# Attention and experts on one core: own banks for the transposes of single slots, and GpSimd's weight splits placed by the slot that runs

## The chip, the cores and the metric

The kernel runs on 1 core of a Trainium2 chip. The metric is the device time of one execution in microseconds (us). Before the change the median of 3 runs is 1021.44 us (1020.47 to 1024.28).

Engines are named as the profile names them: PE is TensorE (PEld its weight loads), DVE VectorE, ACT ScalarE, POOL GpSimd, SP SyncE; a q behind a name means the engine's queue, which issues DMAs and waits.

## The reference

Attention with rotary positions over 8 x 8 heads of 576 x 64, then a mixture of 8 experts on its 4608 rows of 512. Each row goes to one expert, the one with the largest gate logit:

```python
e_idx = np.argmax(logits, axis=1)
for e in range(E):
    mask = e_idx == e
    h = np.maximum(x[mask] @ w1[e], 0.0)      # 512 -> 1024
    ye = h @ w2[e]                            # 1024 -> 512
    out[mask] = gate_w[mask, None] * eom[mask, e, None] * ye
```

Everything is fp32. The kernel reaches fp32 precision on PE with pairs of a rounded part and its remainder: x = xh + xl, w = wh + wl, and x w is taken as xh wh + xl wh + xh wl.

## The kernel before, in words

Attention takes somewhat more than the first half of the time. The expert part is the class `Moe`. The rows of each expert are cut into **slots**. A double slot holds 256 rows in two halves of 128 and a single slot 128 rows. The list `todo` fixes their order: 26 slots run, numbered 0 to 25, and the singles are 7, 8, 10, 12, 13, 15, 17, 18, 20, 22, 23 and 25; so there are four pairs of singles (7 and 8, 12 and 13, 17 and 18, 22 and 23), three lone singles with a double behind them (10, 15, 20), and the last slot. A further branch for more slots stands behind them.

The weights of a slot come in 8 pieces of 128 x 1024: pieces 0 to 3 are w1, pieces 4 to 7 are w2. Piece j of slot s has the number u = 8 s + j, and the tiles of it are `wr` (loaded), `wh` (rounded part) and `wl` (remainder); wl87 is piece 7 of slot 10.

`slot` (line 1169) writes out the order by hand, in 8 steps, for every engine at once. In step j:

- PE works on piece j. Steps 0 to 3 are `first` (ph, the product with w1, and its relu on ACT), steps 4 to 7 are `second` (py, the product with w2).
- In a single slot relu rows `hr` lie with the tokens on the partitions, so they are turned on PE by `across` (line 1109) in steps 1 to 4: two transposes into `htp`, then ACT rounds them into one half of `ht` and DVE takes the remainder into the other (L1118, L1119). In a double slot L1106 and L1107 do that without a turn.
- `split` (line 1040) is called for piece u + 6: ACT rounds wr to wh (L1047) and one engine takes the remainder wl (L1049). That engine is POOL when the piece is for a single slot and is its piece 1 or 5, and DVE otherwise.
- SP issues the load of piece u + 8 (L1038) as soon as its buffer of eight is read.
- In steps 4 and 5 `turn` brings in the tokens of the next slot: four transposes into `mtp` (L1055), ACT's rounded part and DVE's remainder `xt` (L1070, L1071). A single slot has one such part, a double slot two. The product with w1 of the next slot needs all of `xt`.
- In step 6 POOL issues the gather of the tokens of slot s + 2 (L1025), and in step 7 the stores of this slot's rows (L1144), one for a single and two for a double. A store waits for its rows and for the store before it to land.

So each engine has one queue in the order of these calls, and an instruction waits for all that stand ahead of it on its engine. `Small` hands out PSUM tiles for transposes; in the expert part they come from a pool of two banks, shared by `mtp` and `htp`, and a transpose waits until the tile two before it has been read. `ph` has two banks and the pool `pm` (py) two of four.

```python
eng = self.nc.gpsimd if self.todo[s][0] == 1 and j % 4 == 1 else self.nc.vector   # in split, s and j of the piece
tp = self.small.tile(f"htp{s}_{j}{self.nm}")                                      # in across
self.split(u + self.LEAD)                                                         # in slot, LEAD = 6
```

Of the kernel before, what the change touches and what calls it, by code (L numbers as in the profile page):

```python
# [10 lines left out]
F32 = mybir.dt.float32  # L11
# [12 lines left out]
P = 128  # L24
# [738 lines left out]
class Moe:  # L763
# [273 lines left out]
        self.wr[u] = self.buf("wr", u, self.LOADS, 4, [P, 1024], F32, f"wr{u}{self.nm}")  # L1037
        self.nc.sync.dma_start(out=self.wr[u], in_=self.w[bass.ds(self.regs[s] * P + j * E * P, P), :])  # L1038

    def split(self, u):  # L1040
        if u >= 8 * self.end:
            return
        s, j = divmod(u, 8)
        wh = self.buf("wh", u, self.SPLITS, 3, [P, 1024], F32R, f"wh{u}{self.nm}")
        wl = self.buf("wl", u, self.SPLITS, 3, [P, 1024], F32R, f"wl{u}{self.nm}")
        r = self.wr.pop(u)
        self.nc.scalar.copy(wh, r)  # L1047
        eng = self.nc.gpsimd if self.todo[s][0] == 1 and j % 4 == 1 else self.nc.vector
        eng.tensor_tensor(out=wl, in0=r, in1=wh.bitcast(F32), op=ALU.subtract)  # L1049
        self.wp[u] = (wh, wl)  # L1050

# [58 lines left out]
    def across(self, s, j):  # L1110

        hth, htl = self.ht[s]
        js = slice(2 * j, 2 * j + 2)
        hr = self.hrs.pop((s, j))
        tp = self.small.tile(f"htp{s}_{j}{self.nm}")
        for f in range(2):
            self.nc.tensor.transpose(out=tp[:, f, :], in_=hr[:, f, :], identity=self.ident)
        self.nc.scalar.copy(hth[:, js, 0:P], tp[:, 0:2, :])  # L1118
        self.nc.vector.tensor_tensor(out=htl[:, js, 0:P], in0=tp[:, 0:2, :], in1=hth.bitcast(F32)[:, js, 0:P], op=ALU.subtract)  # L1119
# [51 lines left out]
    def slot(self, s, left, per=2):  # L1171
        for j in range(8):
            u = 8 * s + j
            single = self.todo[s][0] == 1
            if j < 4:
                if s or j > 1 or not self.n0:
                    self.first(s, j)
            else:
                self.second(s, j - 4)
            if single and 1 <= j <= 4:  # L1180
                self.across(s, j - 1)
            self.split(u + self.LEAD)
            self.load(u + self.LOADS)
            if j in (4, 5):
                self.turn(s + 1, j - 4)
            if j == 7:
                self.store(s)
            if j == 6:
                self.gather(s + 2)
            for _ in range(per if s or j > 1 else 1):  # L1190
                if left:
                    left.pop(0)()
# [64 lines left out]
```

## Time and profile before

| | |
|---|---|
| median of 3 runs | 1021.44 us (1020.47 to 1024.28) |
| profiled execution: its time, its span | 1019.95 us, 1018.1 us |
| PE, DVE, ACT, POOL busy over the span | 94%, 80%, 61%, 59% |
| splits of weights on DVE, on POOL | 184, 24 |
[...]

The page gives shares over the whole span, while the change lies in the expert part alone, from about 560 us on. So the table is only a start: what counts is read from single slots, by windows cut at the slots' borders, by what PE waits for there, and by the instructions of DVE, ACT and POOL in order of time.

### The profile page before, as it was taken

The numbers are of one execution on the slowest core, as the hardware profiler recorded it, in microseconds if no ns is written. First come the engines' busy times: TensorE is split into PE (matmuls) and PEld (weight loads), VectorE is DVE, ScalarE is ACT, GpSimd is POOL, SyncE is SP. The second block draws the span as 40 slices with busy tenths as digits, with TensorE's granted clock in tenths as the row PEclk, the third lists the DMA queues.
The fourth block names the chain that finished last, engine by engine and source line by source line (L and its number), as shares of the span: only waits on it lengthen the run. The fifth ranks groups of instructions, "written<-read, shape, count | busy, mean of one in ns | idle before, by whom it ended". The sixth has DMA issues, their size and how long they took to land.

```text
span 1018.1 us, 34712 instructions
## 1 busy us (share of the span) xinstructions
PE 960.7 (94%) x14461; PEld 841.7 (83%) x14461; DVE 812.5 (80%) x1262; ACT 621.2 (61%) x1300; POOL 601.0 (59%) x620
## 2 busy tenths in 40 slices
PE   4999999989999999999889999999999999999995
PEld 4778888878878788887788888898998989898894
DVE  6789989989899999999759777667677776867772
ACT  4566666656666666666545455458567765856762
POOL 4677998898988989989521112135315243542621
PEclk9999999999999999999999999999999999999998
DMA  6555665575746748555569767658787877977860
GB/s 223 158 160 155 185 201 147 168 213 150 230 117 198 212 124 239 168 170 146 183 215 337 269 205 238 219 196 306 284 300 238 332 282 255 348 271 275 288 245 29
DMA packets 58208, 221.00 MB, mean 217 GB/s; under 512 B 9351, under 2 KB 9660, under 8 KB 53952
## 3 DMA queue, kind: packets, MB, share of 16 engines
q1 hardware_dynamic: 50304, 196.37, 60.8%
q0 software_dynamic: 6464, 21.26, 5.4%
q8 instruction: 115, 1.88, 0.8%
q10 hardware_dynamic: 1280, 1.11, 0.3%
q14 instruction: 45, 0.37, 0.1%
HBM read 198.64 MB, written 22.43 MB: 217 GB/s over the span
## 4 chain that ended last, share of the span: by engine, by line
PE 70%; POOL 10%; DVE 8%; issue 6%; ACT 5%; DMA 1%; ACTq 0%; POOLq 0%; SPq 0%; DVEq 0%
PE py L1132 18%; PE sc L491 16%; PE ph L1090 15%; PE acc L533 10%; PE ph L1082 5%; POOL raw L435 4%; PE acc L548 4%; ACT pm L505 3%; DVE m L496 3%; DVE wl L1049 2%; POOL raw L439 2%; PE mtp L1055 2%; POOL q L417 1%; POOL pl L714 1%; ACT wh L1047 1%
## 5 line engine op out<-in xcount | busy, mean ns | idle before, releaser
L505 ACT ACTIVATE pm<-sc,m 128x576 f32<-128x576 f32 x288 | 211.3, 738 | 180.1 <-DVE m L496 176.7
L1049 DVE TENSOR_TENSOR wl<-wr,wh 128x1024 fp32r<-128x1024 f32 x184 | 253.2, 1389 | 44.7 <-ACT wh L1047 43.1
L496 DVE TENSOR_REDUCE m<-sc 128x1 f32<-128x576 f32 x288 | 205.8, 749 | 44.3 <-PE sc L491 43.1
L491 PE MATMUL sc<-kh,q 64*128 64x288 f32 x1024 | 205.3, 324 | 21.4 <-ACT pm L505 9.6
L1132 PE MATMUL py<-wh,ht 128*128 128x512 f32 x640 | 214.3, 399 | 0.0
L1047 ACT CAST wh<-wr 128x1024 fp32r<-128x1024 f32 x208 | 212.5, 1050 | 0.0
L533 PE MATMUL acc<-pt,v 32*64 32x128 f32 (+1 forms) x9216 | 197.2, 296 | 13.0 <-DVE xb L560 8.5
L511 DVE STREAM_TRANSPOSE pt<-pm 128x576 f32<-128x576 f32 x288 | 207.1, 753 | 0.0
L491 PEld LDWEIGHTS sc<-kh,q 64*128 64x128 f32 x1024 | 154.0, 190 | 51.8 <-ACT pm L505 27.7
L533 PEld LDWEIGHTS acc<-pt,v 32*64 32x64 f32 x9216 | 157.8, 131 | 38.3 <-issue 22.2
L435 POOL TENSOR_TENSOR raw<-raw,rt 128x1152 f32<-128x1152 f32 x62 | 164.1, 2647 | 0.2
L1090 PE MATMUL ph<-xt,wh 128*128 128x256 f32 x896 | 160.9, 282 | 0.5 <-DVE xt L1071 0.5
L1090 PEld LDWEIGHTS ph<-xt,wh 128*128 128x128 f32 x896 | 138.2, 189 | 2.7 <-DVE xt L1071 1.5
L1132 PEld LDWEIGHTS py<-wh,ht 128*128 128x128 f32 x640 | 120.2, 188 | 24.0
L491 PE MATMUL sc<-kl,q 64*128 64x288 f32 x512 | 129.7, 306 | 0.0
L1090 PE MATMUL ph<-xt,wl 128*128 128x256 f32 x448 | 125.8, 281 | 0.0
L1132 PE MATMUL py<-wl,ht 128*128 128x512 f32 x320 | 125.0, 391 | 0.0
L1049 POOL TENSOR_TENSOR wl<-wr,wh 128x1024 fp32r<-128x1024 f32 x24 | 58.7, 2444 | 89.0 <-ACT wh L1047 75.2
L439 POOL TENSOR_TENSOR raw<-raw 128x576 f32<-128x576 f32 x62 | 88.0, 1419 | 1.8
L1106 ACT ACTIVATE ht<-ph 128x512 fp32r<-128x512 f32 x56 | 33.5, 598 | 88.0 <-PE ph L1090 88.0
L491 PEld LDWEIGHTS sc<-kl,q 64*128 64x128 f32 x512 | 86.1, 191 | 0.4 <-DVE kl L417 0.2
L1090 PEld LDWEIGHTS ph<-xt,wl 128*128 128x128 f32 x448 | 84.5, 189 | 0.1
(248 smaller groups left out, 1308.2 us busy)
## 6 DMA issues: line engine op xcount, KB each, us to landing
wr<-in_w SPq DMA_DIRECT2D x208, 512.0 KB, 5.3
raw<-in_qk SPq DMA_DIRECT2D x64, 576.0 KB, 4.7
v<-in_v SPq DMA_DIRECT2D x128, 288.0 KB, 5.4
xd<-xb SPq DMA_DIRECT2D x16, 640.0 KB, 6.4
xd<-xb SPq DMA_DIRECT2D x8, 160.0 KB, 4.4
rt<-in_rope ACTq DMA_DIRECT2D x1, 576.0 KB, 5.5
xg<-xd,2idx POOLq DMA_INDIRECT x18, 7.1
out<-y,2idx POOLq DMA_INDIRECT x18, 5.2
```

The lines of the kernel that those rows point to most:

```text
L435: self.eng(eng).tensor_tensor(out=rv, in0=rv, in1=self.rt[:, 2 * t:2 * t + 2, x], op=ALU.mult)
L439: self.eng(eng).tensor_tensor(out=r[:, 2 * t, x], in0=r[:, 2 * t, x], in1=r[:, 2 * t + 1, x], op=ALU.add)
L491: self.nc.tensor.matmul(self.ps[i][:, a, :HS], st, mov[r, x], start=(n == 0), stop=(n == 2))
L496: nc.vector.tensor_reduce(self.m[i], ps[:, :, :HS], axis=AX.XY, op=ALU.max, negate=True)
L505: nc.scalar.activation(pe.rearrange("p (a b) -> p a b", a=2), self.ps[i][:, :, :HS], AF.Exp, bias=self.m[i], scale=1.0, accum_out=self.z[: ...
L511: self.nc.vector.transpose(out=self.pt[:, st[0] + 5 * st[1] if st else 4, :], in_=self.pc.pop(i))
L533: nc.tensor.matmul(self.acc[h * D:h * D + D, a, o:o + 32 * n], self.v[r, h, j, :], self.pt[r, u:u + n, 32 * j:32 * j + 32], start=(j == 0) ...
L1047: self.nc.scalar.copy(wh, r)
L1049: eng.tensor_tensor(out=wl, in0=r, in1=wh.bitcast(F32), op=ALU.subtract)
L1082: nc.tensor.matmul(ph[:, 0, :], st[:, dc, 0:P], mv[:, dc, :], start=(n == 0), stop=(n == 11))
L1090: nc.tensor.matmul(ph[:, f, :], st[:, dc, fs], mv[:, dc, :], start=(n == 0), stop=(n == 11))
L1132: self.nc.tensor.matmul(py[h], st[:, f, hs], mv, start=(f == 0 and n == 0), stop=(f == 7 and n == 2))
```

## The change

It does two things. The transposes of `across` no longer use the two shared banks: they take two tiles, htp0 and htp1, in the pool `pm`, which fills its four banks. And `split` no longer chooses its engine by the slot that the piece is for: POOL takes the remainder in steps 1 and 4 of a single slot that is running, so of its own piece 7 and of piece 2 of the slot behind it.

```diff
-    def split(self, u):
+    def split(self, u, help=False):
...
-        eng = self.nc.gpsimd if self.todo[s][0] == 1 and j % 4 == 1 else self.nc.vector
+        eng = self.nc.gpsimd if help else self.nc.vector
...
-        tp = self.small.tile(f"htp{s}_{j}{self.nm}")
+        tp = self.pm.tile([P, 4, P], F32, tag=f"htp{j % 2}", name=f"htp{s}_{j}{self.nm}")
...
-            self.split(u + self.LEAD)
+            self.split(u + self.LEAD, single and j in (1, 4))
```

POOL's queue from the stores of slot 6 (y6) to that of slot 8 (y8), the first pair of singles. xg is a gather of tokens, out a store.

```order
 L1144 DMA out_0<-y6_12076,2idx_11216 4608x512 x2
-L1049 TENSOR_TENSOR wl65_12190<-wr65_12141,wh65_12189 128x1024
-L1025 DMA xg_9501<-xd_83,2idx_11216 128x640 x2
-L1049 TENSOR_TENSOR wl69_12261<-wr69_12234,wh69_12260 128x1024
+L1049 TENSOR_TENSOR wl63_12138<-wr63_12074,wh63_12137 128x1024
+L1049 TENSOR_TENSOR wl66_12208<-wr66_12167,wh66_12207 128x1024
+L1025 DMA xg_9501<-xd_83,2idx_11216 128x640 x2
 L1144 DMA out_0<-y7_12266,1idx_11566 4608x512
+L1049 TENSOR_TENSOR wl71_12324<-wr71_12264,wh71_12323 128x1024
+L1049 TENSOR_TENSOR wl74_12394<-wr74_12353,wh74_12393 128x1024
 L1025 DMA xg_9501<-xd_83,1idx_11566 128x640
```

In slot 7 the two splits now stand ahead of the gathers for slot 9, with none between these and the store of slot 7, and slot 8, which had no split on POOL, has two. Over all slots POOL has 23 splits and DVE 185.

DVE's queue in slot 10, a lone single, from its step 0 to the second half of slot 11's tokens, as it is with the change.

```order
L1049 TENSOR_TENSOR wl86_12722<-wr86_12669,wh86_12721 128x1024
L1119 TENSOR_TENSOR ht1_10_12705<-htp10_0_12751,ht0_10_12704 128x2x128
L1119 TENSOR_TENSOR ht1_10_12705<-htp10_1_12777,ht0_10_12704 128x2x128
L1049 TENSOR_TENSOR wl88_12783<-wr88_12734,wh88_12782 128x1024
L1119 TENSOR_TENSOR ht1_10_12705<-htp10_2_12803,ht0_10_12704 128x2x128
L1049 TENSOR_TENSOR wl89_12809<-wr89_12760,wh89_12808 128x1024
L1119 TENSOR_TENSOR ht1_10_12705<-htp10_3_12821,ht0_10_12704 128x2x128
L1064 COPY gs11_12834<-xg_9501 128x2
L1071 TENSOR_TENSOR xt1_11_12833<-mtp11_0_12836,xt0_11_12832 128x4x128
L1049 TENSOR_TENSOR wl91_12850<-wr91_12812,wh91_12849 128x1024
L1071 TENSOR_TENSOR xt1_11_12833<-mtp11_1_12855,xt0_11_12832 128x4x128
```

Before, wl87 stood between the first two remainders of relu rows and wl90 ahead of the copy gs11; both are on POOL now. The last instruction shown stands behind wl89 and wl91 as before.

PE in slot 8, where the tokens of slot 9 are turned; the waits are named by engine or DMA queue.

```order
-L1055 MATMUL mtp9_0_12403<-ident_91,xg_9501 128x128 [waits DMASW0_49,DVE_49]
+L1055 MATMUL mtp9_0_12403<-ident_91,xg_9501 128x128 [waits DMASW0_49]
 L1055 MATMUL mtp9_0_12403<-ident_91,xg_9501 128x128 x3
 L1132 MATMUL py8_0_12381<-wh69_12260,ht0_8_12271 128x512
-L1132 MATMUL py8_0_12381<-wl69_12261,ht0_8_12271 128x512 [waits Pool_49]
+L1132 MATMUL py8_0_12381<-wl69_12261,ht0_8_12271 128x512
```

The order of PE's instructions is unchanged. The transposes of tokens wait for the gather alone now, and no longer for DVE to have read a tile of relu rows.

## Rows read from the trace of the kernel before

**Rows 1.** Slots 7 to 10: length, busy us of PE, PEld, DVE, ACT, POOL (instructions)
```profile
689.76:702.35 12.59, 12.59 (x86) 11.47 (x86) 9.09 (x12) 10.74 (x18) 6.24 (x4) 1.00 0.79 267
702.35:716.02 13.67, 13.21 (x90) 11.85 (x90) 12.57 (x16) 12.08 (x20) 6.93 (x4) 1.00 0.99 382
716.02:738.88 22.86, 22.86 (x150) 20.81 (x150) 13.94 (x14) 11.86 (x15) 10.06 (x5) 1.00 0.76 268
738.88:751.87 12.99, 12.99 (x89) 11.65 (x88) 10.59 (x15) 11.18 (x19) 3.04 (x3) 1.00 0.82 289
```
**Rows 2.** Waits of PE and its weight loads, 640 to 1010 us (total, times, longest)
```profile
PE mtp L1055 <- DVE ht L1119: 2.5, 4, 0.8
...
PEld mtp L1055 <- DVE ht L1119: 3.5, 4, 1.1
PEld ph L1090 <- DVE xt L1071: 0.6, 3, 0.2
```
**Rows 3.** Instructions on the tile wl: duration in ns, least, median, most
```profile
L1049 DVE TENSOR_TENSOR wl<-wr,wh x184: 1203/1224/3451, 514.3 to 999.3; 128x1024 fp32r<-128x1024 f32 x184
L1049 POOL TENSOR_TENSOR wl<-wr,wh x24: 2388/2444/2506, 680.0 to 990.1; 128x1024 fp32r<-128x1024 f32 x24
```
**Rows 4.** Order of time, DVE and POOL where their splits meet (start, us, instruction, idle before)
```profile
701.76 2.35 DVE L1049 TENSOR_TENSOR wl<-wr,wh 128x1024 fp32r<-128x1024 f32 x2
703.90 2.47 POOL L1049 TENSOR_TENSOR wl<-wr,wh 128x1024 fp32r<-128x1024 f32 x1
705.21 2.24 DVE L1049 TENSOR_TENSOR wl<-wr,wh 128x1024 fp32r<-128x1024 f32 x1 [1.10 <-ACT wh L1047]
...
684.05 4.55 DVE L1049 TENSOR_TENSOR wl<-wr,wh 128x1024 fp32r<-128x1024 f32 x2
685.08 2.44 POOL L1049 TENSOR_TENSOR wl<-wr,wh 128x1024 fp32r<-128x1024 f32 x1 [0.70 <-ACT wh L1047]
...
953.68 2.45 POOL L1049 TENSOR_TENSOR wl<-wr,wh 128x1024 fp32r<-128x1024 f32 x1
953.87 0.42 DVE L1119 TENSOR_TENSOR ht<-htp,ht 128x256 fp32r<-128x256 f32 x1 [0.71 <-ACT ht L1118]
```
**Rows 5.** Order of time in slot 10: POOL, DVE, ACT, and PE's weight loads
```profile
744.87 0.98 POOL L1144 DMA_INDIRECT out<-y,2idx  x1 [4.65 <-DVE wl L1049]
745.02 1.23 DVE L1049 TENSOR_TENSOR wl<-wr,wh 128x1024 fp32r<-128x1024 f32 x1
746.71 1.23 DVE L1049 TENSOR_TENSOR wl<-wr,wh 128x1024 fp32r<-128x1024 f32 x1
750.00 1.22 DVE L1049 TENSOR_TENSOR wl<-wr,wh 128x1024 fp32r<-128x1024 f32 x1
751.14 0.69 DVE L1071 TENSOR_TENSOR xt<-mtp,xt 128x512 fp32r<-128x512 f32 x1
...
747.11 1.05 ACT L1047 CAST wh<-wr 128x1024 fp32r<-128x1024 f32 x1
...
751.88 0.19 PEld L1090 LDWEIGHTS ph<-xt,wh 128*128 128x128 f32 x1 [0.20 <-DVE xt L1071]
```
**Rows 6.** Order of time in slots 7 and 8: POOL, DVE, ACT
```profile
695.66 0.98 POOL L1144 DMA_INDIRECT out<-y,2idx  x1 [4.57 <-DVE wl L1049]
700.24 1.85 POOL L1025 DMA_INDIRECT xg<-xd,2idx  x1 [0.16 <-issue]
702.39 1.48 POOL L1025 DMA_INDIRECT xg<-xd,2idx  x1 [0.30 <-issue]
706.52 1.82 POOL L1144 DMA_INDIRECT out<-y,1idx  x1 [0.15 <-issue]
...
695.92 1.23 DVE L1049 TENSOR_TENSOR wl<-wr,wh 128x1024 fp32r<-128x1024 f32 x1
...
707.41 1.06 ACT L1047 CAST wh<-wr 128x1024 fp32r<-128x1024 f32 x1
710.61 1.05 ACT L1047 CAST wh<-wr 128x1024 fp32r<-128x1024 f32 x1
```

## The prediction

> **What bounds the kernel now.** The change touches single slots only, so I read the windows cut at the borders of slots 7 to 10 first [rows 1]. PE is busy in all of slot 7 (12.59 of 12.59 us), slot 9 and slot 10, and in 13.21 of 13.67 us of slot 8. So PE sets the pace there, and only slot 8, the second of a pair of singles, has a hole. The reader should also see the columns of DVE: 12.57 of 13.67 us in slot 8 and 10.59 of 12.99 in slot 10, against 13.94 of 22.86 in slot 9, a double. DVE is nearly full exactly where the change adds to what it may have to wait for.
>
> The waits of PE say what the hole is [rows 2]: over all 26 slots PE waits for `mtp` behind DVE's read of a tile of relu rows 4 times, 2.5 us in all, 3.5 us by the weight loads. Four is the number of pairs. Nothing else makes PE wait there but 0.6 us for `xt`, three times 0.2, as at 751.88 ahead of slot 11 [rows 5]. That small row matters: DVE's last piece of the next tokens ended at 751.14 + 0.69 = 751.83 and PE took it at once. Behind a lone single, DVE has no slack left.
>
> **Part 1, the banks.** The transposes of tokens lose their wait for DVE. That takes away 2.5 us if nothing else comes late, 3.5 at most [rows 2]. It adds no instruction. But the tokens' remainder is still taken by DVE in its own order, so the gain holds only if DVE delivers `xt` as much earlier.
>
> [...]
>
> **Part 2, the splits.** A split takes 2.44 us on POOL and 1.22 on DVE [rows 3]. What counts is how they meet [rows 4]:
>
> - A DVE split reached while POOL's runs is held to its end and ends 1.08 us after it: POOL 703.90 + 2.47 = 706.37, DVE 705.21 + 2.24 = 707.45.
> - A POOL split reached while DVE's runs is held likewise and ends 2.26 us after it: the DVE pair of 701.76 ends at 704.11, POOL at 706.37.
> - Who waits first is served first: the second DVE split of the two from 684.05 (4.55 us, against 2.35 for such a pair alone) let the POOL split of 685.08 pass, and lost 2.20 us. I take it that a waiting DVE split likewise passes a second POOL split.
> - DVE instructions that read PSUM are not held: the one at 953.87 took 0.42 us in the middle of a POOL split. These are `ht` and `xt`.
>
> So a POOL split removes 1.14 us from DVE (the step from 750.00 to 751.14 [rows 5]) and costs it up to 2.2 us of waiting if DVE is full. In doubles this was paid out of idle time; there DVE now gets all eight splits and no hold, which costs nothing under 22.86 us of PE [rows 1]. In singles there is no such cover. [...]
>
> *A lone single (slots 10, 15, 20).* I put the new order on the rows of slot 10 [rows 5]. The first POOL split, wl87, stands behind the second store, which ends at 744.87 + 0.98 = 745.85, long after its cast. DVE is in wl88 until 745.02 + 1.23 = 746.25, so wl87 ends at 746.25 + 2.26 = 748.51. wl89, which ran from 746.71, ends at 748.51 + 1.08 = 749.59 instead of 747.94. The second POOL split, wl90, has its cast at 747.11 + 1.05 = 748.16 and waits behind wl89: 749.59 + 2.26 = 751.85. DVE meanwhile does the remainder of relu rows and the first half of the tokens, then reaches wl91 and is held: 752.93 instead of 751.22. The second half of slot 11's tokens follows, 0.08 before that end and 0.69 long: 753.54 instead of 751.83. PE waits **1.7 us**. Three such slots: 5.1 us.
>
> *A pair (7 and 8, and three more).* Same rules [rows 6]. The store ends at 696.64, DVE's wl64 at 695.92 + 1.23 = 697.15, so wl63 on POOL ends at 699.41, wl65 on DVE at 700.49, wl66 on POOL at 702.75, wl67 on DVE at 703.83. That harms nothing in slot 7 itself: the one token half of slot 8 is ready near 701.5, before 702.35. Three more DVE splits of 1.14 bring DVE to 707.25, two remainders of relu rows to 708.0. POOL has the two gathers and the store ahead of its next split: 702.75, and as long as from 700.24 to 703.87, and 1.82, and three gaps of some 0.2 make 708.5. DVE's next split, wl72, has its cast at 707.41 + 1.06 = 708.47. So both arrive together, and there are two cases.
>
> - DVE first: wl72 709.71, wl71 on POOL 711.97, wl73 713.05, wl74 on POOL 715.31, wl75 716.39, the last half of the tokens 717.0.
> - POOL first: wl71 710.90, wl72 711.98, wl74 (cast at 710.61 + 1.05 = 711.66) 714.24, wl73 715.32, the remainder of the relu rows and half the tokens some 0.95, wl75 717.4, the last half 718.0.
>
> Slot 9 began at 716.02 [rows 1], with the `mtp` hole in it. It would begin at 717.0 or 718.0: **1.0 to 2.0 us** later, the gain of part 1 already used up. I take 1.5, the middle, since the tie can fall either way. Four pairs: 6 us.
>
> Slot 25 has one POOL split left and no slot behind it: nothing.
>
> **The sum.** 5.1 + 6.0 = 11.1 us more. The profiled execution took 1019.95 us, so 1031 for it; the median of the runs is 1.5 us above it, 1021.44, so **1032 us**. The ends of the costs: 3 x 1.7 + 4 x 1.0 = 9 and 3 x 1.7 + 4 x 2.0 = 13.
>
> **Rivals.**
>
> *The holes close and nothing opens (not slower).* One mechanism: POOL's splits fall into the time in which DVE waits for casts, DVE has its two splits fewer per single, `xt` comes in time, and PE saves its 2.5 to 3.5 us: 1018 to 1019 us. The place that decides is the last half of the tokens of slot 11: it must be there by 751.9. For it speaks that DVE is idle 2.4 us in slot 10; against it, that this idle time lies ahead of the point where POOL is freed by its store (745.85). [...] 6 in 100.
>
> *Only the second hold counts.* If POOL's second store came some 2 us earlier (its wait there is 4.65 us behind the store before [rows 5]), wl87 would be over early. Then wl90 from 748.16 meets wl89 until 748.4, ends near 750.6, wl91 near 751.7, the tokens near 752.3: 0.5 us a lone single, and nothing or the saved 0.6 in a pair. 1020 to 1024 us. POOL is off PE's path now, so little pulls the store forward: 9 in 100. Something between this and the forecast, 1024 to 1029: 12 in 100.
>
> *POOL's lateness reaches further (worse).* The buffer of slot 7's last piece, wr63, is free when POOL ends at 699.41; before, DVE had read it ahead of wl64, by 695.92 [rows 6]. The load into it, the cast of that piece and ACT's queue behind the cast can shift by up to those 3.5 us, as can the two gathers, now behind wl66. The trace of before has no row in which ACT waits for a load or PE for a gather, so the price lies between 0 and 3.5 us a pair; it decides where the store that frees POOL lands latest. With POOL first in every pair, and half the pairs at the middle of that, 1.7, the sum is 5.1 + 8 + 3.4 = 16.5 us: 1038. 18 in 100.
>
> **How the numbers follow.** The forecast with its own range, 1029 to 1036, has 55 in 100. Half a per cent, 5.1 us, is about what a measurement of this kernel tells from no change. Faster by more than that is out of reach of both parts (at most 3.5 us): 2 in 100, for what I do not see. Within it lie the first two rivals: 15. The rest, 83, is slower. The range that leaves out no more than 2 in 10 runs from 1024, above the first two rivals, to 1041, above the worst.
>
> **What would show it.** In the new profile PE's wait for `mtp` behind DVE is gone. In its place PE waits for `xt` L1071 ahead of the doubles behind singles, seven times, by 1 to 2 us each; POOL's 23 splits lie in single slots, and DVE splits that meet them take up to 3.4 us. Slots 7 and others that are followed by a single keep their length, doubles theirs. It is wrong if DVE's splits in singles are not held, if PE's wait for `xt` stays under 0.5 us in slot 11, or if PE waits for casts or gathers instead.

## The result and the profile after

The changed kernel takes 1033.03 us (median of 6 runs, 1030.97 to 1036.22); the kernel before, run beside it, 1023.33 us (6 runs, 1020.47 to 1027.79). The ratio is **1.0096** (95% interval 1.0067 to 1.0124): 0.7 to 1.2% slower, and the medians differ by 9.7 us. The profiled execution took 1030.97 us with a span of 1029.2, 11.1 us more than the span before, at a mean granted clock of 0.993 (before: 0.997). One run of e1 below took 2976.96 us, far from all others, and is left out there.

To find where, I cut PE's rows at the first product with w1 of each slot. The **expert part**, from slot 0's first product to the last product with w2 of slot 25, took 486.1 us before (520.8 to 1006.9 us of the trace) and 497.0 after: 10.95 of the 11.1 us. The differences in the lengths of slots, after less before:

| slots | first single | second single | double behind | together |
|---|---|---|---|---|
| 7, 8, 9 | -0.04 | -0.27 | +1.29 | +0.98 |
| 12, 13, 14 | -0.02 | -0.30 | +1.41 | +1.09 |
| 17, 18, 19 | -0.03 | -0.63 | +1.43 | +0.77 |
| 22, 23, 24 | -0.02 | -0.65 | +1.52 | +0.85 |
| 10, 11 (lone) | +1.49 | | +2.78 | +4.27 |
| 15, 16 (lone) | -0.01 | | +1.34 | +1.33 |
| 20, 21 (lone) | -0.04 | | +1.66 | +1.62 |

Slots 0 to 6 and 25 differ by 0.05 at most. The windows of slots 7 to 11 of the changed kernel (length, busy us of PE, PEld, DVE, ACT and POOL, granted clock) answer to [rows 1]:

```profile
689.78:702.33 12.55, 12.55 (x86) 11.48 (x84) 8.96 (x10) 10.69 (x18) 7.36 (x5) 1.00 0.64 200
702.33:715.73 13.40, 13.24 (x90) 11.86 (x88) 12.34 (x14) 11.81 (x20) 9.74 (x6) 1.00 0.97 362
715.73:739.88 24.15, 23.05 (x150) 20.73 (x148) 16.56 (x18) 11.90 (x16) 4.18 (x4) 1.00 0.88 314
739.88:754.36 14.48, 13.23 (x89) 11.75 (x88) 10.91 (x11) 11.44 (x19) 8.69 (x5) 1.00 0.50 172
754.36:780.04 25.68, 24.59 (x149) 22.28 (x148) 16.55 (x18) 11.68 (x15) 3.03 (x2) 0.93 0.74 260
```

The hole in slot 8 has shrunk from 0.46 to 0.16 us, and holes have opened in slots 9, 10 and 11. The waits of PE and of its weight loads in the changed kernel, from 640 us on (total, times, longest), say what they are:

```profile
PEld ph L1090 <- DVE xt L1071: 10.8, 7, 1.8
PE ph L1090 <- DVE xt L1071: 8.6, 7, 1.5
...
PE py L1132 <- DVE ht L1119: 1.3, 1, 1.3
PE ph L1082 <- DVE xt L1071: 0.5, 3, 0.2
```

The wait for `mtp` behind DVE [rows 2] is gone. In its place PE waits seven times, once ahead of each double behind a single, for DVE's last half of the tokens. The splits of the changed kernel by engine, beside [rows 3]:

```profile
L1049 DVE TENSOR_TENSOR wl<-wr,wh x185: 1203/1219/3406, 514.8 to 1008.7; 128x1024 fp32r<-128x1024 f32 x185
L1049 POOL TENSOR_TENSOR wl<-wr,wh x23: 2390/2419/2797, 694.8 to 1010.8; 128x1024 fp32r<-128x1024 f32 x23
```

All 23 of POOL's splits now lie in single slots, and 22 of them meet splits of DVE. Sorted by the two rules of the prediction, the rows show one picture: where DVE is held, its end is 1.08 or 1.09 us behind POOL's; where POOL is held, its split ends 2.27 to 2.29 us behind DVE's.

**What the prediction had not seen** stands in the rows of DVE and POOL of the changed kernel at the end of slot 8, in order of time:

```profile
712.31 2.40 POOL L1049 TENSOR_TENSOR wl<-wr,wh 128x1024 fp32r<-128x1024 f32 x1 [2.44 <-ACT wh L1047]
...
712.35 0.41 DVE L1119 TENSOR_TENSOR ht<-htp,ht 128x256 fp32r<-128x256 f32 x1
712.68 2.05 DVE L1064 COPY gs<-xg 128x2 f32<-128x2 f32 x1
714.65 0.68 DVE L1071 TENSOR_TENSOR xt<-mtp,xt 128x512 fp32r<-128x512 f32 x1
715.25 1.21 DVE L1049 TENSOR_TENSOR wl<-wr,wh 128x1024 fp32r<-128x1024 f32 x1
716.38 0.68 DVE L1071 TENSOR_TENSOR xt<-mtp,xt 128x512 fp32r<-128x512 f32 x1
```

DVE's copy of the gates, `gs`, 2 numbers a partition, takes 2.05 us and ends at 714.73, 0.02 behind POOL's split. It stands ahead of both halves of the tokens. The row above it, `ht` from PSUM, is not held (0.41). Over the whole kernel the copy's durations are, before and then after:

```profile
L1064 DVE COPY gs<-xg x26: 152/156/414, 513.0 to 988.5; 128x2 f32<-128x2 f32 x26
```
```profile
L1064 DVE COPY gs<-xg x26: 149/163/2064, 513.5 to 998.3; 128x2 f32<-128x2 f32 x26
```

Ten of the 26 copies take 2.03 to 2.06 us after the change, the others 0.15 to 0.17. Six of the ten stand ahead of a double, in slots 8, 13, 15, 18, 20 and 23; the other four, in slots 7, 12, 17 and 22, stand ahead of a second single, where PE waits 0.2 us at most.

**Slot 10 is a case of its own.** POOL's and DVE's rows of the changed kernel there:

```profile
745.76 2.42 POOL L1049 TENSOR_TENSOR wl<-wr,wh 128x1024 fp32r<-128x1024 f32 x1
749.45 2.41 POOL L1049 TENSOR_TENSOR wl<-wr,wh 128x1024 fp32r<-128x1024 f32 x1 [1.27 <-issue]
...
746.18 3.09 DVE L1049 TENSOR_TENSOR wl<-wr,wh 128x1024 fp32r<-128x1024 f32 x1 [0.53 <-ACT wh L1047]
749.20 0.41 DVE L1119 TENSOR_TENSOR ht<-htp,ht 128x256 fp32r<-128x256 f32 x1
749.53 3.41 DVE L1049 TENSOR_TENSOR wl<-wr,wh 128x1024 fp32r<-128x1024 f32 x1
752.87 0.41 DVE L1119 TENSOR_TENSOR ht<-htp,ht 128x256 fp32r<-128x256 f32 x1
```

POOL came first both times, the second time by 0.08 us (749.45 against 749.53), so DVE lost nearly 2 us and then 2.2. The last remainder of relu rows, at 752.87, is then late as well as the tokens. PE and the windows behind it in the changed kernel:

```profile
753.33 0.74 PE L1132 MATMUL py<-wh,ht 128*128 128x512 f32 x2 [1.25 <-DVE ht L1119]
...
755.73 0.38 PE L1090 MATMUL ph<-xt,wh 128*128 128x256 f32 x1 [1.09 <-DVE xt L1071]
```
```profile
755.50:760.00 4.50, 4.27 (x23) 4.27 (x24) 2.44 (x3) 0.00 (x0) 3.03 (x2) 0.62 0.92 347
760.00:764.00 4.00, 4.00 (x36) 4.00 (x36) 2.17 (x3) 2.41 (x4) 0.00 (x0) 1.00 0.62 245
```

PE was idle for 1.25 and for 1.09 us within 4 us, and from 756.0 to 759.4 us the granted clock stood at 0.5 of full speed; in the 4.5 us of the first window that leaves a mean of 0.62, and 0.38 x 4.5 = 1.7 us lost. That is most of slot 11's +2.78, which stands against +1.34 and +1.66 for slots 16 and 21.

### The profile page after: what moved, and what is told of

Its sections match the earlier page's. It is cut to its first block, busy times and chain, and to the rows that moved or that the text cites. A ratio compares the mean times of both kernels' runs of the same rounds, so it can differ in the third digit from the quotient of the medians.

```text
span 1029.2 us, 34702 instructions
## 1 busy us (share of the span) xinstructions
PE 964.7 (94%) x14461; PEld 844.2 (82%) x14461; DVE 814.6 (79%) x1263; ACT 619.6 (60%) x1300; POOL 588.1 (57%) x619
## 4 chain that ended last, share of the span: by engine, by line
PE 62%; DVE 10%; POOL 10%; issue 9%; ACT 6%; DMA 1%; ACTq 0%; POOLq 0%; DVEq 0%
PE sc L491 16%; PE ph L1090 13%; PE py L1132 13%; PE acc L533 10%; PE ph L1082 5%; PE acc L548 4%; ACT pm L505 4%; POOL raw L435 4%; DVE wl L1049 3%; DVE m L496 3%; POOL raw L439 2%; ACT wh L1047 1%; POOL q L417 1%; DVE xt L1071 1%; POOL pl L714 1%
## 5 line engine op out<-in xcount | busy, mean ns | idle before, releaser
L1049 DVE TENSOR_TENSOR wl<-wr,wh 128x1024 fp32r<-128x1024 f32 x185 | 234.4, 1290 | 36.1 <-ACT wh L1047 34.8
L1090 PE MATMUL ph<-xt,wh 128*128 128x256 f32 x896 | 163.6, 284 | 9.2 <-DVE xt L1071 9.2
L1144 POOL DMA_INDIRECT out<-y,2idx x18 | 19.4, 1079 | 198.0 <-ACT y L1141 173.7
```

The costliest lines, as they stand in the source:

```text
L1090: nc.tensor.matmul(ph[:, f, :], st[:, dc, fs], mv[:, dc, :], start=(n == 0), stop=(n == 11))
```

## The experiments

Theories at the start. **A**, that of the prediction: POOL's splits in singles hold DVE, and `xt` is late by it. Rivals: **B**, the banks of their own cost something themselves; **C**, the banks are a gain of 2.5 us and the splits hide it; **D**, DVE is overfull in singles and needs more help from POOL, not less; **E**, POOL's own lateness (stores, gathers, the buffer it reads) makes the loss. Below, "expert part" is that of each profiled execution, against 486.1 us before and 497.0 after.

**e1: the banks alone.** The kernel before, with this line changed.

```diff
-        tp = self.small.tile(f"htp{s}_{j}{self.nm}")
+        tp = self.pm.tile([P, 4, P], F32, tag=f"htp{j % 2}", name=f"htp{s}_{j}{self.nm}")
```

> Only the banks of part 1, splits as before. Theory A (DVE is held by GpSimd's splits in single slots, the banks are harmless): PE loses its wait for mtp behind DVE (2.5 us), but the tokens' second half ended at 715.72 in slot 8 where PE would now be ready near 715.4, so about 0.3 us a pair is kept: -1 us, -2.5 at most, against before. Theory B (the banks cost the time): +8 to +11 us. Theory C (banks are what was short): the whole -2.5 us.

Measured: 1022.85 us, ratio 1.0006 (0.9987 to 1.0026), expert part 485.45. The wait for `mtp` is gone, and the waits of PE hold this instead:

```profile
PE ph L1090 <- DVE xt L1071: 2.1, 4, 0.7
```

The second singles are 0.6 to 1.0 us shorter, the doubles behind them 0.5 to 1.0 longer. The four waits of [rows 2] have moved one step down the chain, from DVE's `ht` to DVE's `xt`. B falls, since it costs nothing. C expected 2.5 us here and falls with nothing; that the old splits do not hide such a gain is seen in e3 and e4, where no split is on POOL and the banks are worth 0.1 us (483.2 against 483.4).

**e2: the splits alone.** The changed kernel with the line of e1 turned back.

> Only part 2, the splits by the slot that runs, transposes of relu rows in the shared banks. Theory A: as the change or a little more, +9 to +13 us against before, PE waiting for xt ahead of the doubles behind singles. Theory B (the banks cost the time): within 2 us of before.

Measured: 1032.4 us, ratio 1.0104 (1.0076 to 1.0132), expert part 499.4. The loss is there without the banks. Its waits are mostly for `mtp`, not for `xt` as was expected:

```profile
PE mtp L1055 <- DVE ht L1119: 10.7, 12, 2.0
PE ph L1090 <- DVE xt L1071: 2.3, 6, 0.4
```

The banks thus do what was said of them, they end the wait for `mtp`, and in the expert part that is worth 2.3 us while DVE is held (499.4 against 497.0, which has 1.7 us of half clock in it that e2 lacks); the medians of the two kernels, 1032.4 and 1033.0, don't tell it.

**e3 and e4: no split on POOL**, with the banks of their own (e3, the changed kernel) and with shared banks (e4, the kernel before with the new `split` and the same call).

```diff
-            self.split(u + self.LEAD, single and j in (1, 4))
+            self.split(u + self.LEAD)
```

> The change with no split on GpSimd at all: DVE takes all 208. Theory A: nothing holds DVE, PE's wait for mtp is gone and xt is in time but for the 0.2 us behind lone singles: -2.5 us against before, some 12 below the change. Theory D (DVE has simply too much work in single slots, help is needed): each single has two splits of 1.14 us more than with the change, so 1 to 2 us later still at each of 7 doubles, +15 us or more against before.

> No split on GpSimd and the shared banks of before. Theory A: without the holds of 0.8 and 1.0 us in a pair DVE reads the relu rows about 1 us earlier in the second single, so most of the four waits for mtp go too: -1 to -2.5 us against before, within 1.5 us of the kernel that has the banks as well. Theory C: the waits for mtp stay, 0.

Measured: e3 1017.41 us, ratio **0.9931** (0.9901 to 0.9961), expert part 483.2; e4 1018.92 us, ratio **0.9966** (0.9946 to 0.9986), expert part 483.4. Neither trace lists a wait of PE's products for DVE (the weight loads wait for `xt` seven times, 0.3 us at most). The splits of e3:

```profile
L1049 DVE TENSOR_TENSOR wl<-wr,wh x208: 1203/1225/1233, 513.5 to 997.3; 128x1024 fp32r<-128x1024 f32 x104
```

All 208 on DVE, and the longest takes 1.233 us. D falls: with 24 splits more than before DVE is in time everywhere. Both kernels are faster than either of the study. In e4 the wait for `mtp` is gone although the banks are shared, so what [rows 2] showed as a shortage of banks was a hold by POOL that ended at the bank. Of the medians' gain of e3 (5.7 us against the kernel before, run beside it at 1023.13) the expert part shows 2.9; the rest isn't explained by slots, and e3 and e4 are not told apart by their intervals.

**e5 and e6: one of the two splits.** The changed kernel with POOL's split in step 1 only, and in step 4 only (`single and j == 1`, `single and j == 4`).

> The change with GpSimd's split in step 1 of a single alone; DVE takes that of step 4. Theory A: one hold of 2.2 us and one split of 1.14 more on DVE, so each of 7 doubles begins up to 1 us earlier than with the change: +2 to +8 us against before. Theory E (GpSimd's lateness in its own queue costs the time, loads and gathers behind it): about half of the change's cost in either of the two halves, +5.

> The change with GpSimd's split in step 4 alone. Theory A: a lone single is 0.5 us late by the same working (the split meets only the last DVE split ahead of the tokens), a pair gains its 0.6 or nothing: -1 to +3 us against before. Theory E: as the half with step 1, +5.

Measured: e5 1025.47 us, ratio 1.0025 (1.0009 to 1.0040), expert part 488.1; e6 1025.89 us, ratio 1.0029 (1.0012 to 1.0045), expert part 490.1, of which 0.95 lies in slot 0 at half clock, far from any split. Against e3 that is 4.9 and 6.0 (without the half clock) us; both splits together cost 13.8 (e3 against the changed kernel). So the two cost 3 us more than their sum, 10.8. Slots 10 and 11 have 2.0 of it: +1.7 in e5 and +0.5 in e6 over the kernel before, +4.27 in the changed kernel, where the stretch of half clock lies. A's ranges were +2 to +8 and -1 to +3 against before. e5 lies at the lower end of its own (+2.8 in the medians, +2.0 in the expert part), e6 just above its own (+3.2, and +3.1 in the expert part without the half clock); E's +5 for either is met by neither. The waits of PE in e6 also hold a row that no trace above has:

```profile
PE mtp L1055 <- DMA xg<-xd,2idx: 1.7, 4, 0.5
```

With the pair's gathers queued behind POOL's split (in slot 7 at 702.14, its gathers at 704.72 and 706.87), PE waits for them four times. This is what E said, at 0.4 us a time.

**e7 and e8: POOL busy with something else.** All splits on DVE, banks of their own. In steps 1 and 4 of each single, e7 lets POOL write a scratch tile of 128 x 1024 bf16 numbers three times; e8 lets it multiply that tile by itself.

```diff
+            if single and j in (1, 4):
+                self.aside()
```
In `aside` stands the first of these pieces in e7, the second in e8:

```diff
+        for _ in range(3):
+            self.nc.gpsimd.memset(self.scr, 0.0)
```
```diff
+        self.nc.gpsimd.tensor_tensor(out=self.scr, in0=self.scr, in1=self.scr, op=ALU.mult)
```

> All splits on DVE, and in steps 1 and 4 of a single GpSimd instead clears a scratch tile three times: it only writes. Theory A (what holds DVE is GpSimd's reading): no DVE split is longer than 1.25 us in singles, the time is that of the kernel with all splits on DVE, within 1.5 us. If any GpSimd work holds DVE: its splits grow as under the change and the time is 10 us or more above that kernel.

> All splits on DVE, and in steps 1 and 4 of a single GpSimd multiplies a scratch tile with itself, 128 x 1024: it reads as a split does, takes nothing off DVE and touches no buffer that a load or a cast waits for. Theory A: the same holds with two splits of 1.14 us more on DVE in each single, so 2 to 3 us later than with the change at each of 7 doubles: +18 to +28 us against before. Theory E (GpSimd's late results and buffers cost the time): as the kernel in which GpSimd only writes.

Measured: e7 1019.88 us, ratio 0.9983 (0.9962 to 1.0004), expert part 483.2; e8 1053.62 us, ratio 1.0299 (1.0276 to 1.0322), expert part 518.4. POOL's added work, e7 and then e8, by line and shape, and the splits of e8:

```profile
L1176 POOL MEMSET scr<- 128x1024 bf16 x72 | 68.8, 955 | 3.5
```
```profile
L1175 POOL TENSOR_TENSOR scr<-scr 128x1024 bf16<-128x1024 bf16 x24 | 56.3, 2346 | 1.2
```
```profile
L1049 DVE TENSOR_TENSOR wl<-wr,wh x208: 1202/1221/3495, 513.2 to 1030.3; 128x1024 fp32r<-128x1024 f32 x104
```

POOL is busy longer in e7 (68.8 against 56.3 us) from the same two steps, DVE's longest split is 1.27 us (1.25 was expected; e4, without any work on POOL there, has 1.268), and the expert part is that of e3 (the median is 2.5 us over e3's, which no slot shows). In e8, where POOL reads, DVE is held up to 3.5 us. POOL's being late or busy (E) doesn't make the loss, as e7 shows; the multiplication of e8, which reads SBUF, does (up to 3.495 us for a split of DVE, against 1.270 in e7). The two runs differ in the operation as well as in its reading, and no run takes these apart. e8 lost more than the change, and more than was expected of it: DVE has all splits there and is held too, and five stretches of half clock came on top.

**e9, e10 and e11: the small copy on ScalarE**, in the changed kernel, in e6 and in e3. Theory **G**, formed on the rows of slot 8 above: a part of the loss is the hold of the `gs` copy, not that of the splits.

```diff
-            V.tensor_copy(self.gss[s], self.xgs[s % 2][:, :, P])
+            nc.scalar.copy(self.gss[s], self.xgs[s % 2][:, :, P])
```

> The changed kernel with the small copy of the gates (gs, line 1064, 128x2 numbers) on ScalarE instead of VectorE. Theory G: GpSimd's step-4 splits hold this copy too (ten of the 26 copies took 2.03 to 2.06 us in the changed kernel, 0.16 us elsewhere), and the subtractions of xt stand behind it. With the copy gone from VectorE xt0 runs at once, the split behind it is held instead until 1.08 us after GpSimd's end, and xt1 comes about 0.6 us sooner: 0.6 at each of the 7 places where TensorE waits for xt, 3 to 5 us in all (more if the stretch of half clock in slot 11 goes, 1.6): the expert part 491 to 494 us instead of 497.0, the run 1027 to 1030 us, no DVE copy over 0.5 us in the trace. Rival: the split behind the copy takes the whole hold over, and xt1 is as late as before: 496 to 498 us, the run 1032 to 1034. Rival: ScalarE's extra copies cost more than they give: over 498 us.

> The changed kernel with GpSimd's splits in step 4 alone (the run before of that kind had its expert part at 490.1 us, about 0.95 of it a stretch of half clock in slot 0) and the small copy of the gates on ScalarE. There four of the copies took 1.43 to 1.74 us. Theory G: the four doubles behind a pair win 0.4 to 0.6 us each, so the expert part is 487 to 488.5 us and the run 1022.5 to 1025. Rival (the split takes the hold over): no more than the 0.95 of the clock is won, 489 to 490.5 us, the run 1025 to 1026.5.

> All splits on VectorE, the banks of their own, and the small copy of the gates on ScalarE: the control for the two runs beside it. GpSimd runs no split here, so nothing can hold the copy, and its move is worth 0.16 us of VectorE 26 times, which nobody waits for. Expected the expert part of the kernel with all splits on VectorE, 483.2 plus or minus 0.5 us, and the run 1016 to 1019.5 us. If the move itself costs ScalarE's row of casts something, it shows here as over 484 us.

Measured: e9 1030.61 us, ratio 1.0080 (1.0054 to 1.0106), expert part 495.0; e10 1024.40 us, ratio 1.0011 (0.9985 to 1.0036), expert part 488.0; e11 1018.89 us, ratio 0.9952 (0.9927 to 0.9977), expert part 482.3, 0.4 below what was expected. The move itself costs nothing, by e11. The waits of PE in e9:

```profile
PE mtp L1055 <- DMA xg<-xd,2idx: 4.2, 4, 2.6
PE ph L1090 <- DVE xt L1071: 3.4, 5, 1.0
PE py L1132 <- DVE ht L1119: 1.3, 1, 1.3
```

PE's wait for `xt` falls from 8.6 to 3.4 us, a gain of 5.2, just over the 3 to 5 that G gave. But the expert part is only 2.1 us shorter, 1 us short of G's range, and the run is 0.6 us above its 1027 to 1030: the gathers of the tokens came late four times, once by 2.6 us in slot 18. The second gather of a pair is issued 2.06 to 2.22 us into the second single in e9, against 1.24 to 1.33 in the changed kernel; why is not shown. PE's rows there:

```profile
886.52 0.40 PE L1132 MATMUL py<-wh,ht 128*128 128x512 f32 x1
889.49 1.12 PE L1055 MATMUL mtp<-ident,xg 128*128 128x128 f32 x4 [2.58 <-DMA xg<-xd,2idx]
```

A stretch of half clock follows that gap too (889.5 to 892.9), and slot 18 is 3.2 us longer than before. In slot 11 the half clock is gone. In e10 the expert part lands within G's range; of the 2.1 us against e6, 0.95 is the half clock in slot 0 that e10 lacks. The four doubles behind pairs are 0.24 to 0.61 us shorter than in e6, and PE's wait for `xt` falls from 3.0 to 1.3 us. Here too the gathers took some of it back: slot 23, with a wait of 0.9 us for one, is 0.68 longer than in e6. G holds for the waits; of the time, about half was lost again.

## Why the prediction was right, and where its steps were off

The time (1032 against 1033.03, range 1024 to 1041) and the sum (11.1 against 10.95 us in the expert part) came out, and so did the mechanism. That the sum came out so closely is luck: the lone singles cost 2.1 us more than their term, the pairs 2.3 us less, and 1.7 us of the total is a stretch of half clock that no term holds. Two slips of the working changed nothing: the chances add up to 102, and by the terms named POOL's next split in slot 8 comes to 708.8, not 708.5 (it started at 707.48).

- **Part 1, the banks.** Right that the wait for `mtp` goes, and that "the gain holds only if DVE delivers `xt` as much earlier": e1 shows that it does not, 2.1 us of `xt` for 2.5 of `mtp`. The reading of the four gaps as a shortage of banks (C) falls with e4, which has shared banks and no such wait.
- **Part 2, the holds.** Both rules (1.08 and 2.26) and "who waits first is served first" are in the rows of the changed kernel to 0.03 us, and so is the statement that remainders from PSUM are not held: 21 of `ht` lie wholly within a POOL split there and take 0.41 to 0.43 us, as all 48 do. e2, e3, e7 and e8 show that this is the cause. Incomplete was the list of what is held: the prediction counted splits alone. The copy `gs`, on its own queue ahead of `xt`, is held as well (2.03 to 2.06 us, ten times).
- **Lone singles, 3 x 1.7 = 5.1.** Measured 4.27 + 1.33 + 1.62 = 7.2. In slots 15 and 20 the size is near, by another way than the prediction's: POOL's store was over sooner (835.37 in slot 15, 5.1 us into the slot, against 6.97 for slot 10 before), as the rival "only the second hold counts" had it, which gave 0.5; the held copy made up more than half of the rest, since e9 has +0.86 and +1.02 for slots 16 and 21 where the change has +1.34 and +1.66. In slot 10 POOL came first at both meetings; the prediction had DVE first. That cost 1.25 us in a place that it did not name (`py` behind `ht`), and 1.7 us of clock. In e9 POOL is first at both meetings of slot 10 too (748.90 against 749.05 at the second).
- **Pairs, 4 x 1.5 = 6.** Measured 0.98 + 1.09 + 0.77 + 0.85 = 3.7: the size was at and below the lower end of 1.0 to 2.0. The step that failed is the start of the chain. The prediction took the end of the store, 696.64, from [rows 6]; here POOL's first split starts at 694.83:

```profile
693.73 1.09 POOL L1144 DMA_INDIRECT out<-y,2idx  x1 [2.47 <-PE htp L1117]
694.83 2.43 POOL L1049 TENSOR_TENSOR wl<-wr,wh 128x1024 fp32r<-128x1024 f32 x1
...
696.10 2.25 DVE L1049 TENSOR_TENSOR wl<-wr,wh 128x1024 fp32r<-128x1024 f32 x1 [0.52 <-ACT wh L1047]
```

So POOL's split was first and unhindered, DVE was held by it once and not pushed on through four splits in turn.

The store waits for the store before it to land, and that came sooner: in slot 6 the first store took 4.8 us from issue to landing before and 2.7 after, and the second started 0.76 us behind that landing both times. In the eight doubles ahead of a single the second store starts 3.5 us behind the first in the changed kernel (4.4 in slot 9), against 4.8 to 6.1 before (3.5 in slot 24). That belongs to the change: by the pages of the profiles the stores `out<-y,2idx` took a median of 5.2 us from issue to landing before and in e1, which has POOL's splits by the old rule, and 2.8 to 3.7 in the changed kernel and the other ten, with POOL's splits in singles or with none. The traces also show what lies beside it. These are the 1.7 us behind the first store of slot 6 before, of slot 6 after, and of slot 24 before; the last number but one is the busy share of the DMA engines:

```profile
691.09:692.79 1.70, 1.70 (x17) 1.70 (x16) 0.23 (x1) 1.47 (x3) 0.00 (x0) 1.00 0.99 323
691.26:692.96 1.70, 1.70 (x17) 1.70 (x15) 0.23 (x1) 1.46 (x3) 0.00 (x1) 1.00 0.38 157
996.10:997.80 1.70, 1.70 (x16) 1.70 (x16) 0.20 (x1) 1.44 (x3) 0.04 (x1) 1.00 0.38 154
```

Before, a POOL split met DVE's in the double itself (684.05 and 685.08 in [rows 4]), so two buffers of weights came free late, and SP issued their loads 1.45 and 0.82 us ahead of the first store of slot 6; the loads and the store then ran at the same time. After the change the last load there is issued 3.4 us ahead of the store. In the six other doubles ahead of a single, slot 24 left aside, the share is likewise 0.98 to 1.05 before and 0.38 to 0.43 after. In slot 24 no load is left, and there the second store came after 3.5 us before the change too. The prediction moved the splits and left the loads, and with them the stores, where the old splits had put them; its sentence that little pulls the store forward is what was wrong.

- **The rival "POOL's lateness reaches further"** is a real mechanism, by gathers rather than by the buffer: 1.7 us in e6, 4.2 in e9, 2.1 in e10. It isn't in the changed kernel, whose second gather of a pair is issued 1.24 to 1.33 us into the second single, against 1.75 to 1.81 in e6.

Two things stay open. That the loads make the stores land late is read from the traces, not shown by a run that moves the loads alone, and they don't explain the 4.4 us of slot 9. And whether slot 10's second meeting falls to POOL in every execution of the changed kernel wasn't tried; by 0.08 us it need not.

## What to carry to other kernels

A second engine that takes a share of the work is a gain only if it doesn't lock the first one out: count what it saves (here 1.14 us of DVE a split) against what it holds (up to 2.2), and for every instruction that may meet it, not only for those of the same kind. A wait at a bank does not say that banks are short: follow back what keeps the reader of the bank, as e1 and e4 did here, where the cure of the symptom gave nothing and moving the helper's work back gave 0.3 to 0.7%. When a wait is taken away, look for the next thing that PE needs and price it before counting the gain.

## What was unexpected of the hardware

- A copy of 128 x 2 numbers on DVE can cost 2.05 us instead of 0.16, when POOL's split runs beside it. Beside POOL's writes alone (e7) the same copy took up to 0.54, while DVE's splits stayed at 1.27 or less.
- Two idle gaps of PE of 1.25 and 1.09 us close together, and a single one of 2.58 (e9), were each followed by some 3.4 us at a granted clock of 0.5, at a price of 1.7 us, more than either gap of the first case. Lone gaps of up to 1.5 us in the changed kernel and of 1.61 in e5 were not, nor were two of 1.25 and 1.01 in slots 10 and 11 of e9 and two of 2.01 and 1.29 in slot 10 of e2. Of e8's seven gaps of 2.04 to 2.23 us four were. What tips it is not shown here.
- A store landed later where weight loads ran beside it: in the doubles ahead of singles POOL's second store came 4.8 to 6.1 us behind the first where they did (before), and 3.5, once 4.4, where they did not (after).
- In e8 the recorded starts do not tell who is first: DVE's split began at 750.10, POOL's multiplication at 750.59, and yet DVE's ended 1.09 us after POOL's. For the splits the recorded order and the hold agree in every meeting of the changed kernel.
